# Early values, later weights and filler transposes in the first batch of a pooled-attention and two-MoE kernel

## Chip, cores and metric

The kernel runs on one core of a Trainium2 chip. The metric is the device time of one execution in microseconds; the median of three runs is given. The engines are called as in the profile: PE (TensorE), DVE (VectorE), ACT (ScalarE), POOL (GpSimd) and SP, the queue that issues all transfers here.

## What is computed

Three stages follow each other: attention with pooled queries, a two-matrix MoE, and a second MoE with three input matrices. Batch 4, 8 heads, 1152 keys, head size 64; after pooling 576 queries a head.

```python
q_pool = q.reshape(B, H, S // 2, 2, D).mean(axis=3)
attn = softmax(1 / sqrt(D) * q_pool @ k.T)      # per head
x = (attn @ v)                                  # -> (2304, 512)
h = x @ w_in;  x = max(0.01 * h, h) @ w_out     # 512 -> 2048 -> 512
h = max(max(x @ w1, x @ w2), x @ w3)            # 512 -> 768
out = h @ w2_out                                # 768 -> 512
```

All of it is float32. The weights reach the device as 64-bit floats, viewed as pairs of 32-bit integers, and are decoded there.

## The kernel before

**Batches and pairs.** The heads are taken two at a time: 4 batches of 4 pairs, numbered n = 0 to 15. The attention of a batch runs pair by pair; the two MoE stages of a batch (`experts`) run as filling between the key tiles of the next batch's attention, and those of the last batch run alone at the end. So the attention of the first batch (n = 0 to 3, `n < NP`) has no matmuls of an MoE beside it.

**One pair.** A pair has two phases (320 and 256 query columns a head) of nine key tiles. `prep_q` and `prep_k` transpose queries and keys on PE (tiles `psq`, `psk`), and ACT and DVE split them into a rounded and a rest part. `scores` makes one tile of 128 query rows by 1152 keys with 6 matmuls of 384 columns (tile `s`), DVE takes the row maximum (`mx`, L299 to L309), ACT the exponential (`p`, L302, L305, L310). `probs_t` then handles one key tile: it takes a PSUM bank, transposes four 128x128 blocks of `p` into it (tile `pst`) and lets ACT copy the bank to SBUF (`pt`, L352). `probs_m` does the same for the fifth score tile with three transposes (`psf`, copied by DVE at L361). After three key tiles `values` multiplies by v: 12 matmul records on tile `pv`. `evac` scales and stores the result.

**Slots.** A key tile is a slot. `at(slot, ...)` hangs the next pair's scores, preparations and loads on slots of the current one. `load_v` of the next pair stands on the last slot of the first phase; two `v` buffers take turns. Before the change, eight weight chunks (`PRE = 8`) are hung on slots of the first batch with `predecode`.

**Weights.** There are 56 chunks of 512 KB. `decoded` (L546) loads the raw integers (`wraw`, L551) and turns them into floats with four DVE operations (L561, L564, L567, L571), one on ACT (L570) and one on POOL (L574); `split_chunk` splits the result on ACT (L587) and POOL (L588) into tile `wsplit`, of which a copy is stored to DRAM (L596). Later batches, and chunks that were predecoded, load the split copy back (`w`, L610). There are two raw buffers, two buffers for the decoded floats and five for split chunks (`w_p`). The first two raw loads wait for the first `values` (`GATE`).

**Who sets the order.** The code is recorded in program order, and the tile framework's scheduler then orders each engine's instructions; every engine and the SP queue works its list strictly in that order. `on_pe` (L106 to L120, the line of all matmuls and transposes is L109) only keeps the matmuls of one `values` group together.

Of the kernel before, what the change touches and what calls it, by code (L numbers as in the profile page):

```python
# [7 lines left out]
F32 = mybir.dt.float32  # L8
F32R = mybir.dt.float32r
# [13 lines left out]
def kernel(  # L23
# [22 lines left out]
    B, H, S, D = q.shape  # L46
    T = S // 2
    NP = H // 2
    KT = S // 128
    QP = 72  # L50
    QC = T // QP
    KDM = moe_w_in.shape[0] // 128
# [6 lines left out]
    TM = 512  # L59
# [1 line left out]
    TR_ = B * REST  # L61
    PG = 3
    FREE = 2 * NP
    PRE = 8
    scale = 0.5 / float(D) ** 0.5
    NOSYNC = mybir.DependencyInfo(mybir.DependencyClass.NoSync, mybir.DependencyReason.DATA)

# [3 lines left out]
    vs_p = ctx.enter_context(tc.tile_pool(name="vs", bufs=2))  # L71
# [6 lines left out]
    x_p = ctx.enter_context(tc.tile_pool(name="x", bufs=X_BUFS))  # L78
    g_p = ctx.enter_context(tc.tile_pool(name="g", bufs=6))
    acc_p = ctx.enter_context(tc.tile_pool(name="acc", bufs=1))  # L80
# [13 lines left out]
    ident = const.tile([128, 128], F32, name="ident")  # L94
# [11 lines left out]
    def on_pe(f, *args, **kwargs):  # L106


        mm = f(*args, **kwargs)  # L109
        if grouped[0]:  # L110
            for other in between:
                tc.add_manual_dep(mm.ins, other.name, NOSYNC, reason="values of a group stay together")
            between.clear()
        if behind[0] is not None:
            tc.add_manual_dep(mm.ins, behind[0].name, NOSYNC, reason="values of a group stay together")
        if grouped[0]:
            behind[0] = mm.ins
        else:
            between.append(mm.ins)
        return mm  # L120

    def transpose(out, in_, eye):
        return on_pe(nc.tensor.transpose, out, in_, eye)
# [7 lines left out]
    def bank(name):  # L131
        turn[0] += 1
        pool = ps_w["m"] if ps_w and turn[0] % 2 == 0 else ps_m
        return pool.tile([128, 512], F32, tag="m", name=name)
# [13 lines left out]
    def gap(j):  # L148
        return X0 - 64 * j

    def spare_tiles():
        for j in range(2):
            for part in range(2):
                t = g_p.tile([128, 2, TM], F32R, tag="g", name="qspare")
                t = t.rearrange("p a t -> p (a t)")
                nc.gpsimd.memset(t[:, gap(j):gap(j) + 64].bitcast(F32), 0.0)
                spare[j, part] = t
        for j in range(2):
            t = x_p.tile([128, 2, T], F32R, tag="x", name="kspare")
            spare[j] = t.rearrange("p a t -> p (a t)")  # L160
# [4 lines left out]
    def load_pair(n):  # L165
        b, hp = divmod(n, NP)
        h0 = 2 * hp
        qr = raw_p.tile([QP, 2, QC, 2, D], F32, tag="q", name="qraw")
        kr = raw_p.tile([128, 2, KT, D], F32, tag="k", name="kraw")

        def load_q(j0, j1):
            nc.sync.dma_start(
                out=qr[:, j0:j1].rearrange("p h c r d -> p h (c r) d"),
                in_=q[b, h0 + j0:h0 + j1].rearrange("h (p c) d -> p h c d", p=QP),
            )

        def load_k(j0, j1):
            nc.sync.dma_start(out=kr[:, j0:j1], in_=k[b, h0 + j0:h0 + j1].rearrange("h (p c) d -> p h c d", p=128))

        for j0, j1 in ((0, 1), (1, 2)) if n == 0 else ((0, 2),):  # L180
            load_q(j0, j1)
            load_k(j0, j1)
        raws[n] = [qr, kr]

    kts = {}
    vss = {}

    def load_v(n):
        b, hp = divmod(n, NP)
        h0 = 2 * hp  # L190
        vss[n] = vs_p.tile([128, 2, KT, D], F32, tag="v", name="v")
        nc.sync.dma_start(out=vss[n], in_=v[b, h0:h0 + 2].rearrange("h (p c) d -> p h c d", p=128))

    def pool_q(n, j0=0, j1=2):
        qr = raws[n][0][:, j0:j1]
        for e in range(2):
            engine = nc.vector if n == 0 and j0 == 0 else nc.gpsimd
            a = [qr[:, :, e::2, r] for r in range(2)]
            engine.tensor_tensor(out=a[1 - e], in0=a[0], in1=a[1], op=ALU.add)
# [142 lines left out]
    def probs_t(n, ph, kt):  # L342
        g = kt % PG
        if g == 0:
            pts[kt // PG] = pt_p.tile([128, PG, 2 * X0], F32, tag="pt", name="pt")
        w = (X0, T - X0)[ph]
        ps = bank("pst")
        for i in range(4):
            p = ptl[n, ph, i].rearrange("p a b -> p (a b)")
            transpose(ps[:, i * 128:(i + 1) * 128], p[:, kt * 128:(kt + 1) * 128], ident)  # L350
        dst = pts[kt // PG][:, g, 0:2 * w].rearrange("p (j c) -> p j c", j=2)[:, :, 0:256]
        nc.scalar.copy(out=dst, in_=ps.rearrange("p (j c) -> p j c", j=2))  # L352
# [67 lines left out]
    def attention():  # L420
        npair = B * NP
        load_pair(0)
        for j in range(2):
            pool_q(0, j, j + 1)
            prep_q(0, j)
            prep_k(0, j)
            if j == 0:
                for i in range(2):
                    scores(0, 0, i)
                    normalise(0, 0, i)  # L430
        load_v(0)
        load_pair(1)
        spare_tiles()
        for i in range(2, 5):
            scores(0, 0, i)
            normalise(0, 0, i)
        phases = [(n, ph) for n in range(npair) for ph in range(2)]
        todo = {}

        def at(slot, cost, f, *args):  # L440
            todo.setdefault(slot, []).append((f, args, cost))

        def now(slot):
            spent = 0
            for f, args, cost in todo.pop(slot, []):
                f(*args)
                spent += cost
            return spent

        for u, (n, ph) in enumerate(phases):  # L450
            s0 = u * KT
            if u + 1 < len(phases):
                nxt = phases[u + 1]
                for i, s in enumerate((FIRST_AT if n < NP else S_AT)[nxt[1]]):
                    at(s0 + s, QK * 6 * (1 + (i == 4)), scores, *nxt, i)
                    at(s0 + s + 1, 0, normalise, *nxt, i)
            if ph == 0 and n + 2 <= NP:
                at(s0 + 6, 0, load_pair, n + 2)
            if ph == 0 and n + 1 < npair:
                at(s0 + 1, 0, pool_q, n + 1)  # L460
                when = PREP_AT[n + 1 > NP]
                for j in range(2):
                    at(s0 + when[2 * j], TR * 3, prep_q, n + 1, j)
                    at(s0 + when[2 * j + 1], TR * 4, prep_k, n + 1, j)
                at(s0 + 8, 0, load_v, n + 1)
            if ph == 1 and n + 1 < npair:
                if n + 2 < npair and n + 2 > NP:
                    at(s0 + 6, 0, load_pair, n + 2)
            if n < FREE:
                at(s0 + 4, TR * 2, spread, n, ph)  # L470
        if wide:
            for c in range(PRE):
                at(6 + c * (2 * NP * KT - 8) // PRE, 0, predecode, c)

        late = []

        def follow():
            pn, pph, pgr = late.pop()
            values(pn, pph, pgr)
            if pgr == KT // PG - 1:  # L480
                last = pn % NP == NP - 1
                if pph == 0 and last:
                    yield "room"
                evac(pn, pph)
                if pph == 1 and last:
                    yield "batch"
            return PG * 4 * (X0, T - X0)[pph] / 2400 + 0.565

        for s in range(len(phases) * KT):
            n, ph = phases[s // KT]  # L490
            gr, g = divmod(s % KT, PG)
            done = 0
            want = CHAIN
            if s == 2 * NP * KT:
                done += yield from follow()
            probs_t(n, ph, gr * PG + g)
            done += TR * 4
            if g == PG - 1 and ph == 0:
                probs_m(n, gr)
                done += TR * PG  # L500
                want -= TR * PG
            c = now(s)
            if g == 0 and late:
                c += yield from follow()
            done += c
            yield done, max(0, want - c)
            yield 0, None
            if g == PG - 1:
                late.append((n, ph, gr))
        yield from follow()  # L510
        assert not todo
# [137 lines left out]
    class Main:  # L649
        n = TM  # L650
# [11 lines left out]
    class Rest:  # L662
        n = TR_
# [179 lines left out]
```

## Time and profile before

| | |
|---|---|
| median of 3 runs | 1404.29 us (1402.0 to 1404.84) |
| the profiled execution, its own time | 1402.59 us |
| its span, first to last instruction | 1400.8 us |
| PE busy | 1282.2 us (92%) |
| PE weight loads busy | 1025.2 us (73%) |
| DVE busy | 711.9 us (51%) |
| ACT busy | 637.1 us (45%) |
| POOL busy | 362.2 us (26%) |
| mean granted PE clock | 0.959 |

Busy times are means over very different stretches: the first batch's attention (to about 238 us), three batches of attention with an MoE beside them, and the last MoE alone (from about 1156 us). PE's matmuls are pipelined and their ends modelled, so PE being busy is not the same as PE being at its best. The granted clock is 1.0 at 2.4 GHz and 0.5 at 1.2 GHz. The "chain" of a window is followed back from its last instruction, at each step to what released it or to the instruction ahead of it on its engine.

### The profile page before, as it was taken

How to read it: one execution, taken by the hardware profiler on the slowest of the kernel's cores; microseconds unless marked ns; L12 is line 12 of the kernel's file. 1: busy time of each engine (PE TensorE's matmuls, PEld its weight loads, DVE VectorE, ACT ScalarE, POOL GpSimd, SP SyncE). 2: the span in 40 equal slices, each digit the busy share in tenths (PEclk: the TensorE clock that was granted, in tenths of full speed). 3: DMA queues.
4: the chain of work that ended last, by engine and by line, in shares of the span. 5: the costliest groups of instructions: out<-in, count | busy, mean ns of one | idle time of the engine just before them, and what ended most of it. 6: DMA issues, size and time to landing. Idle time of an engine off the chain costs nothing.

```text
span 1400.8 us, 19351 instructions
## 1 busy us (share of the span) xinstructions
PE 1282.2 (92%) x7376; PEld 1025.2 (73%) x7376; DVE 711.9 (51%) x1214; ACT 637.1 (45%) x1253; POOL 362.2 (26%) x322
## 2 busy tenths in 40 slices
PE   5778879798898988999999998999999999999998
PEld 4445547676676777778787887778777879888888
DVE  5684553587888777354645452445545411222110
ACT  5676664554555665454545353454444432112111
POOL 1251111354566655021212001120220002224110
PEclk8889889998998999999999999999999999999999
DMA  3473221555555656353535343453533244333343
GB/s 110 143 234 123 72 72 39 145 179 194 173 197 189 222 204 193 129 155 121 156 119 150 120 151 100 150 149 129 153 112 128 102 147 156 121 135 122 106 135 106
DMA packets 88056, 197.51 MB, mean 141 GB/s; under 512 B 11420, under 2 KB 41884, under 8 KB 87964
## 3 DMA queue, kind: packets, MB, share of 16 engines
q1 hardware_dynamic: 87964, 196.28, 43.7%
q8 instruction: 58, 0.95, 0.3%
q14 instruction: 34, 0.28, 0.1%
HBM read 150.99 MB, written 35.13 MB: 133 GB/s over the span
## 4 chain that ended last, share of the span: by engine, by line
PE 70%; DVE 11%; DMA 6%; ACT 5%; issue 4%; POOL 4%; SPq 0%; POOLq 0%; DVEq 0%; ACTq 0%
PE m L109 38%; PE pv L109 10%; PE s L109 9%; PE pst L109 6%; PE o L109 5%; DMA wraw<-in_moe_w_out_dram 3%; DVE mx L309 2%; POOL wmant L574 2%; DMA qraw<-in_q_dram 1%; DVE wraw L564 1%; DMA wraw<-in_moe_w_in_dram 1%; POOL wsplit L588 1%; DVE wmant L561 1%; DVE wmant L567 1%; DVE q L253 1%
## 5 line engine op out<-in xcount | busy, mean ns | idle before, releaser
L109 PE MATMUL m<-x,w 128*128 128x512 f32 x1272 | 321.4, 397 | 0.0
L109 PEld LDWEIGHTS m<-x,w 128*128 128x128 f32 x1272 | 231.6, 188 | 56.3 <-issue 13.6
L352 ACT COPY pt<-pst 128x512 f32<-128x512 f32 x288 | 166.7, 586 | 193.5 <-PE pst L109 192.6
L109 PE MATMUL s<-kt,q 128*128 128x384 f32 x840 | 189.9, 360 | 31.3 <-ACT p L310 14.9
L309 DVE TENSOR_REDUCE mx<-s 128x1 f32<-128x1152 f32 x108 | 146.3, 1355 | 126.6 <-PE s L109 124.3
L109 PE MATMUL pv<-pt,v 128*64 128x256 f32 (+1 forms) x1152 | 184.6, 461 | 15.3 <-DVE pt L361 14.7
L109 PE MATMUL pst<-ident,p 128*128 128x128 f32 x1152 | 179.5, 280 | 20.8 <-DVE pt L361 7.7
L109 PEld LDWEIGHTS pst<-ident,p 128*128 128x128 f32 x1152 | 140.9, 143 | 59.7 <-issue 11.1
L109 PEld LDWEIGHTS s<-kt,q 128*128 128x128 f32 x840 | 149.7, 196 | 43.4 <-ACT p L310 17.4
L709 POOL TENSOR_TENSOR g<-t,g 128x512 fp32r<-128x512 f32 x64 | 84.1, 1314 | 348.4 <-DVE g L708 348.4
L310 ACT ACTIVATE p<-s,mx 128x1152 f32<-128x1152 f32 x108 | 132.3, 1225 | 89.1 <-DVE mx L309 88.3
L109 PE MATMUL m<-g,w 128*128 128x512 f32 x624 | 163.2, 400 | 0.0
L109 PEld LDWEIGHTS pv<-pt,v 128*64 128x64 f32 x1152 | 81.5, 150 | 86.6 <-issue 35.3
L109 PEld LDWEIGHTS m<-g,w 128*128 128x128 f32 x624 | 112.3, 189 | 27.4 <-issue 7.7
L707 ACT ACTIVATE t<-m 128x512 f32<-128x512 f32 x80 | 44.3, 555 | 132.9 <-PE m L109 132.9
L109 PE MATMUL m<-x,wsplit 128*128 128x512 f32 x360 | 98.0, 412 | 0.5 <-ACT pt L352 0.4
L708 DVE CAST g<-t 128x512 fp32r<-128x512 f32 x64 | 30.7, 480 | 112.5 <-ACT t L707 112.0
L588 POOL TENSOR_TENSOR wsplit<-wmant,wsplit 128x512 fp32r<-128x512 f32 x56 | 77.3, 1384 | 35.1 <-ACT wsplit L587 35.1
L574 POOL TENSOR_TENSOR wmant<-wraw 128x512 f32<-128x512 f32 x56 | 64.5, 1153 | 80.3 <-DVE wraw L571 67.9
L647 POOL TENSOR_TENSOR y<-t,y 128x512 fp32r<-128x512 f32 x24 | 31.4, 1310 | 202.0 <-ACT y L646 202.0
L109 PEld LDWEIGHTS m<-x,wsplit 128*128 128x128 f32 x360 | 67.1, 195 | 18.9 <-issue 4.9
L737 DVE TENSOR_TENSOR t<-m,t 128x512 f32<-128x512 f32 (+1 forms) x60 | 38.2, 636 | 83.7 <-PE m L109 72.7
(92 smaller groups left out, 1549.2 us busy)
## 6 DMA issues: line engine op xcount, KB each, us to landing
w<-w SPq DMA_DIRECT2D x176, 512.0 KB, 3.4
w<-wsplit SPq DMA_DIRECT2D x56, 512.0 KB, 3.6
wraw<-in_moe_w_out_dram SPq DMA_DIRECT2D x22, 512.0 KB, 6.1
v<-in_v_dram SPq DMA_DIRECT2D x16, 576.0 KB, 3.7
wraw<-in_moe_w_dram SPq DMA_DIRECT2D x18, 512.0 KB, 4.7
qraw<-in_q_dram SPq DMA_DIRECT2D x15, 576.0 KB
kraw<-in_k_dram SPq DMA_DIRECT2D x15, 576.0 KB, 5.4
q<-q SPq DMA_DIRECT2D x52, 160.0 KB, 2.7
```

The lines of the kernel that those rows point to most:

```text
L109: mm = f(*args, **kwargs)
L253: nc.vector.scalar_tensor_tensor(out=lo, in0=src, scalar=scale, in1=hi, op0=ALU.mult, op1=ALU.subtract)
L309: nc.vector.tensor_reduce(out=mx[:, 0:1], in_=ps[:, :, 0:SN], axis=AX.XY, op=ALU.max, negate=True)
L310: nc.scalar.activation(out=p, in_=ps[:, :, 0:SN], func=ACTF.Exp, bias=mx[:, 0:1], accum_out=rs[:, i:i + 1])
L352: nc.scalar.copy(out=dst, in_=ps.rearrange("p (j c) -> p j c", j=2))
L574: nc.gpsimd.tensor_tensor(out=mf, in0=low.bitcast(F32), in1=high.bitcast(F32), op=ALU.mult)
L588: nc.gpsimd.tensor_tensor(out=t[:, 1], in0=r, in1=t[:, 0], op=ALU.subtract)
L647: nc.gpsimd.tensor_tensor(out=t[:, 1], in0=src, in1=t[:, 0], op=ALU.subtract)
L707: nc.scalar.activation(out=t, in_=ps[:, 0:k.n], func=ACTF.Prelu, alpha=0.01)
L708: nc.vector.tensor_copy(out=gt[:, 0], in_=t)
L709: nc.gpsimd.tensor_tensor(out=gt[:, 1], in0=t, in1=gt[:, 0], op=ALU.subtract)
L737: nc.vector.tensor_tensor(out=t, in0=ps[:, 0:k.n], in1=t, op=ALU.max)
```

## The change

Three edits. `PRE` becomes 0, so no `predecode` is recorded. The v of pairs 1 to 3 are loaded right behind that of pair 0 at the start; for pairs 2 and 3 they lie in buffers that are not used yet (the MoE accumulator and one x tile), and the slots of the first batch no longer load v except that of pair 4. And in the first batch `probs_t` writes four transposes of the identity into its PSUM bank ahead of the four real ones, which overwrite them.

```diff
-    PRE = 8
+    PRE = 0
...
-        vss[n] = vs_p.tile([128, 2, KT, D], F32, tag="v", name="v")
+        if n == 2:
+            t = acc_p.tile([128, KDM, TM], F32, tag="acc", name="vacc").rearrange("p m t -> p (m t)")
+            vss[n] = t[:, 0:2 * KT * D].rearrange("p (h c d) -> p h c d", h=2, c=KT)
+        elif n == 3:
+            t = x_p.tile([128, 2, T], F32R, tag="x", name="vx").bitcast(F32).rearrange("p a t -> p (a t)")
+            vss[n] = t.rearrange("p (h c d) -> p h c d", h=2, c=KT)
+        else:
+            vss[n] = vs_p.tile([128, 2, KT, D], F32, tag="v", name="v")
...
         ps = bank("pst")
+        if n < NP:
+            for i in range(4):
+                transpose(ps[:, i * 128:(i + 1) * 128], ident, ident)
         for i in range(4):
             p = ptl[n, ph, i].rearrange("p a b -> p (a b)")
             transpose(ps[:, i * 128:(i + 1) * 128], p[:, kt * 128:(kt + 1) * 128], ident)
...
         load_v(0)
         load_pair(1)
+        for n in range(1, NP):
+            load_v(n)
         spare_tiles()
...
-                at(s0 + 8, 0, load_v, n + 1)
+                if n + 1 >= NP:
+                    at(s0 + 8, 0, load_v, n + 1)
```

The lists that the scheduler makes show what moves. First PE, in one of the first batch's pairs between two `values` groups (`pst<-ident,p` are real transposes, `pst<-ident` fillers, `s<-kspare,qspare` scores of the next pair). Before:

```order
L109 MATMUL pv<-pt,v 64x320 x6
L109 MATMUL pst<-ident,p 128x128 x4
L109 MATMUL s_117<-kspare,qspare 128x384 x4
L109 MATMUL s_119<-kspare,qspare 128x384 x2
L109 MATMUL pst<-ident,p 128x128 x8
L109 MATMUL pv<-pt,v 64x256 x6
```

The same place after the change:

```order
L109 MATMUL pv<-pt,vacc 64x320 x6
L109 MATMUL pst<-ident 128x128 x4
L109 MATMUL pst<-ident,p 128x128 x4
L109 MATMUL s_117<-kspare,qspare 128x384 x4
L109 MATMUL s_119<-kspare,qspare 128x384 x2
L109 MATMUL pst<-ident 128x128 x4
L109 MATMUL pst<-ident,p 128x128 x4
L109 MATMUL pst<-ident 128x128 x4
L109 MATMUL pst<-ident,p 128x128 x4
L109 MATMUL pv<-pt,vacc 64x256 x6
```

Each key tile has its fillers directly ahead of its real transposes; the rest keeps its order.

Second, the SP queue in the first batch, where the first pair gives way to the second (lines L551 and L564 load raw weights, L596 and L609 store split ones, L610 loads them back, L172 and L178 load q and k, L258 and L265 copy query halves). Before:

```order
L551 DMA wraw<-in_moe_w_in_dram 128x4x256
L596 DMA w_138<-wsplit 128x1024
L172 DMA qraw<-in_q_dram 72x2x1024
L610 DMA w<-w_132 128x1024
L610 DMA w<-w_133 128x1024
L610 DMA w<-w_134 128x1024
L258 DMA q_126<-q_126 64x640
L596 DMA w_139<-wsplit 128x1024
L258 DMA q_127<-q_127 64x640
L610 DMA w<-w_135 128x1024
L551 DMA wraw<-in_moe_w_in_dram 128x4x256
L178 DMA kraw<-in_k_dram 128x2x576
```

After:

```order
L609 DMA w_136<-wsplit 128x1024
L564 DMA wraw<-in_moe_w_out_dram 128x4x256
L564 DMA wraw<-in_moe_w_in_dram 128x4x256
L199 DMA v<-in_v_dram 128x2x576
L265 DMA q_124<-q_124 64x640
L416 DMA xr_128<-x 256x1x64
L265 DMA q_125<-q_125 64x640
L172 DMA qraw<-in_q_dram 72x2x1024
L265 DMA q_126<-q_126 64x640
L265 DMA q_127<-q_127 64x640
L178 DMA kraw<-in_k_dram 128x2x576
```

Raw loads still stand in the first batch's list, since the scheduler moves those of the MoE forward into free buffers: 9 in place of 12, 5 stores in place of 8, and no split chunk is loaded back in place of 5.

Third, DVE at the end of the first pair's decoding. Before, the tenth and last decode of the first batch stands in the middle of the second pair:

```order
L325 RECIPROCAL sums<-sums 128x4
L561 TENSOR_SCALAR wmant<-wraw 128x512
L564 SCALAR_TENSOR_TENSOR wraw<-wraw,wmant 128x512
L567 TENSOR_SCALAR wmant<-wraw 128x512
L299 TENSOR_REDUCE mx<-s_117 128x1
L300 TENSOR_REDUCE mx<-s_119 128x1
L571 SCALAR_TENSOR_TENSOR wraw<-wraw,wmant 128x512
L361 COPY pt<-psf 128x6x64
```

After, the seventh and last (L574 to L584 are the four operations) ends in the first pair:

```order
L574 TENSOR_SCALAR wmant<-wraw 128x512
L577 SCALAR_TENSOR_TENSOR wraw<-wraw,wmant 128x512
L306 TENSOR_REDUCE mx<-s_118 128x1
L580 TENSOR_SCALAR wmant<-wraw 128x512
L307 TENSOR_REDUCE mx<-s_119 128x1
L306 TENSOR_REDUCE mx<-s_117 128x1
L308 TENSOR_REDUCE mx<-mx 128x1
L584 SCALAR_TENSOR_TENSOR wraw<-wraw,wmant 128x512
L307 TENSOR_REDUCE mx<-s_119 128x1
L330 TENSOR_TENSOR sums<-sums 128x5
```

So ten decodes in the first batch become seven, and 46 behind it become 49.

## Rows read from the trace of the kernel before

**Rows 1.** The page, part 2: granted TensorE clock in 40 slices of 35 us, in tenths.

```profile
PEclk8889889998998999999999999999999999999999
```

**Rows 2.** Busy time of each engine in four stretches, one per pair (granted clock behind it).

```profile
41.00:97.00 56.00, 41.74 (x236) 28.01 (x234) 41.80 (x85) 38.84 (x88) 24.49 (x21) 0.84 0.60 185
97.00:149.00 52.00, 40.54 (x241) 27.86 (x241) 29.30 (x62) 31.84 (x75) 8.74 (x9) 0.86 0.46 151
149.00:196.00 47.00, 37.74 (x235) 26.73 (x235) 24.22 (x53) 29.93 (x72) 5.43 (x6) 0.90 0.22 54
196.00:243.00 47.00, 41.38 (x234) 29.55 (x234) 18.37 (x30) 22.95 (x47) 5.40 (x6) 0.89 0.18 47
```

**Rows 3.** The chain that ended last, by line, windows 41:97, 97:149, 149:196, 196:243.

```profile
by line: DMA wraw<-in_moe_w_out_dram 14.7%; DMA wraw<-in_moe_w_in_dram 8.6%; PE pv L109 8.4%; DVE wraw L571 5.9%; POOL wmant L574 5.5%; issue 4.2%; DVE mx L300 4.2%; PE pst L109 4.1%; DVE wmant L561 3.8%; DVE mx L299 3.5%; DVE wraw L564 3.2
by line: DMA wraw<-in_moe_w_in_dram 18.3%; PE pv L109 13.5%; DMA qraw<-in_q_dram 12.4%; PE s L109 10.5%; PE pst L109 6.8%; DVE mx L299 5.4%; ACT p L302 5.0%; ACT pt L352 4.1%; ACT p L305 3.2%; DVE qspare L253 2.8%; DVE mx L300 2.7%; PE psq 
by line: PE pv L109 22.1%; PE s L109 18.1%; PE pst L109 15.8%; ACT pt L352 8.3%; ACT p L302 5.6%; DVE mx L299 4.1%; ACT p L305 3.4%; DVE q L253 3.1%; ACT kt L214 3.0%; DVE kspare L217 3.0%; ACT q L249 2.7%; ACT kspare L214 2.5%; issue 2.1%;
by line: PE pv L109 29.0%; PE s L109 20.5%; PE pst L109 17.3%; PE m L109 14.2%; DVE mx L309 5.8%; DVE kt L217 2.9%; ACT p L310 2.8%; ACT pt L352 2.5%; ACT kt L214 2.5%; issue 1.1%; DVE pt L361 1.0%; PE psr L109 0.5%; PE psq L109 0.5%; DVEq 
```

**Rows 4.** Pieces of that chain, 149:196 (start us, us, what).

```profile
159.20 1.12 PE pst L109 x4
...
164.55 0.45 PE pst L109 x4
...
166.32 1.76 PE pv L109 x12
...
169.72 0.87 PE pst L109 x8
...
177.40 1.45 PE pv L109 x12
...
178.85 1.02 PE pst L109 x8
```

**Rows 5.** Longest pieces of values on that chain, 149:196 and 196:243.

```profile
148.99 3.14 PE pv L109 x12
...
160.32 2.60 PE pv L109 x12
...
196.09 3.40 PE pv L109 x12
...
207.71 2.79 PE pv L109 x12
...
226.79 2.70 PE pv L109 x12
```

**Rows 6.** TensorE in three neighbouring stretches (PE busy, granted clock).

```profile
219.90:223.30 3.40, 2.69 (x20) 1.00 0.00 0
223.30:226.70 3.40, 1.24 (x6) 1.00 0.00 0
226.80:230.20 3.40, 3.40 (x16) 0.50 0.03 7
```

**Rows 7.** The same stretches, instructions on score tiles s alone.

```profile
219.90:223.30 3.40, 1.32 (x6) 1.01 (x6) 0.60 (x1) 1.30 (x2) 1.00 0.00 0
223.30:226.70 3.40, 1.24 (x6) 1.01 (x6) 0.76 (x1) 1.31 (x2) 1.00 0.00 0
```

**Rows 8.** Line L561, first operation of each weight decode, 0:235 and 235:600.

```profile
L561 DVE TENSOR_SCALAR wmant<-wraw x10: 417/427/1028, 49.9 to 113.5; 128x512 int32<-128x512 int32 x10
...
L561 DVE TENSOR_SCALAR wmant<-wraw x46: 409/428/1499, 258.7 to 545.8; 128x512 int32<-128x512 int32 x46
```

**Rows 9.** VectorE in order of time, 108:117 (in brackets: idle before, releaser).

```profile
113.46 0.43 DVE L561 TENSOR_SCALAR wmant<-wraw 128x512 int32<-128x512 int32 x1 [3.37 <-DMA wraw<-in_moe_w_in_dram]
```

**Rows 10.** Busy time of each engine in the second batch's stretch and the third's.

```profile
238.00:587.30 349.30, 309.00 (x1687) 240.04 (x1686) 256.05 (x372) 194.15 (x356) 175.75 (x144) 0.94 0.55 182
587.30:883.80 296.50, 285.35 (x1664) 229.41 (x1663) 146.22 (x257) 134.08 (x251) 44.40 (x34) 0.99 0.43 136
```

## The prediction, as put on record

> **What bounds the kernel now.** The change touches the first batch and, through the decodes that it moves on, the second; so I read the page's strip of slices first and then only those stretches. The strip shows where the granted clock is below full: under 0.9 in most slices of the first 210 us, then in two single slices (315 and 420 us), never behind that [rows 1]. The fillers can only win something where the clock is low.
>
> I cut the first batch into its four pairs, each from its first group of values to the next pair's. They are about 56, 51.5, 47 and 47 us long. No engine is full in any of them: PE is busy 41.7 of 56 us in the first, 37.7 of 47 us in the third, and its clock is 0.84 to 0.90 [rows 2]. So busy shares don't decide, and I went to the chain of waits.
>
> The chain says two different things [rows 3]. In the first pair it runs through the raw weight loads (14.7 and 8.6%) and the decodes on DVE and POOL; the key tiles' transposes (pst) hold 4.1% of it. In the second a raw load still holds 18.3%, and pst 6.8%. In the third and fourth, where nothing is decoded, PE's own work holds more than half, and pst alone 15.8 and 17.3%. There PE's order is the bound, and what is put into PE's list ahead of a real transpose lengthens it.
>
> **The fillers.** 72 key tiles get four more transposes each. Counted on the chain, the key tiles whose transposes lie on it are 3, 7, 13 and 14 of the 18 of each pair: 37 in all. Their shares in rows 3 agree: 4.1% of 56, 6.8% of 52, 15.8% and 17.3% of 47 us are 2.3, 3.5, 7.4 and 8.1 us [rows 3]. Four transposes in a stream take 0.45 us on the chain, eight 0.87 us, so four more cost 0.44 us [rows 4]. 37 x 0.44 = **16.3 us**. The fillers write the same bank as the real transposes, so they wait for that bank as these do and don't run while PE waits for it; the order puts them directly ahead of the real ones in nearly every slot. The other 35 I take at nothing: they lie where PE waits anyway for ACT or DVE to free a score bank or a transposed bank, and if that cover is gone they cost 0.44 us each. Bounds: 0, if all of them moved into waits, and 72 x 0.44 = 31.7 us. In a slow stretch four transposes took 1.12 us [rows 4], so a filler there costs more than twice; I keep the price at full clock because the next term takes the slow stretches back.
>
> **The clock.** What low clock costs on the chain is seen by comparing the same piece at both levels. Twelve values records of the first phase take 1.76 us at full clock, those of the second 1.45 us [rows 4]. In slow stretches the first kind took 3.14, 2.60, 3.40 and 2.79 us, the second 2.70 us [rows 5]. That is 1.4, 0.8, 1.6, 1.0 and 1.25 us lost, and for the pieces at 159 and 207 us 0.5 us more each, for the transposes ahead of them: some 7 us in two pairs. The second pair, once it waits for no weights, would have what the third has, 2.7 us. About 10 us could be won. Which of it do four fillers a key tile win? The slow stretches at 159 and 207 us began right after PE had done little but transposes and two scores with short waits between, a key tile's among them; there fillers add work at the right place, and I take these (1.3 + 1.5 us) and the second pair's like them (1.3) in full: 4.1 us. Those that hold the values at 149 and 196 us began in a longer wait for ACT, with one key tile near; I take half of 1.4 + 1.6 + 1.4, so 2.2 us. The one at 226.8 us followed a wait for ACT without any key tile: nothing. Together **-6.3 us**. Bounds 0 and -10.
>
> Whether transposes keep the clock up at all can be read from the trace. From 219.9 to 223.3 us PE was busy 2.69 us, only 1.32 us of it scores and the rest transposes, and the clock stayed at 1.00 behind it; from 223.3 to 226.7 us it was busy 1.24 us, all scores, and the clock then fell to 0.50 [rows 6, 7]. The two had nearly the same score time; the transposes made the difference. The Trainium skill (TensorE: Matmul & The Clock Gate, Part 4: PE-mode transpose) states that transposes do not count as PE-busy in the same way and that the full clock does not engage for them. By that this term would be 0 and the sum 6.3 us higher; these two stretches speak against it, though two are few.
>
> **The decodes that leave the second pair.** The order shows that the edit does only part of what it says: the scheduler pulls seven decodes forward, all into the first pair, as before; only three go. The first pair therefore stays as it is. In the second, DVE stood 3.37 us waiting for a raw load with a row maximum queued right behind it [rows 9]; five loads back of split chunks, which go too, ran beside it. Without them I expect the pair to take what the third took: 51.5 - 47.1 = 4.4, so **-4.4 us**. But then its chain is PE's like the third's, with 13 key tiles instead of 7: 6 x 0.44 = **+2.6 us**. Bounds of the first: 0, and the raw load's whole 18.3% of 52 us, -9.5.
>
> **The three decodes that arrive in the second batch.** Of the 56, 10 began before 235 us and 46 behind it [rows 8]. The second batch took 349.3 us, the third, with the same matmuls and no decodes, 296.5 us [rows 10]: 52.8 us for 46, 1.15 us each. Three more: **+3.4 us**. Bounds: 0, since DVE is busy 256 of 349 us and has room, and 3 x 7.6 = 22.8 us, if decodes set the pace (349.3 / 46). I stay near the low one, because PE is busy 309 of the 349 us.
>
> **The early v.** Nothing: they stand in SP's list behind the first pair's q and k and ahead of copies that wait for DVE anyway, no values waited for a v load on the chain, and the buffers they borrow are first needed by the MoE or by nobody in this batch. If the cover failed, the first queries would come later by a load or two at the start; I keep no range for it.
>
> **Sum.** 16.3 + 2.6 - 6.3 - 4.4 + 3.4 = +11.6 us. On the profiled execution's own 1402.6 us that is **1414 us**. The median shown is 1.7 us above that execution, inside the spread of the runs, and I leave that out.
>
> **The rivals.**
>
> *Faster: PE stays at full clock and the fillers fall into waits.* For it: in the first batch PE idles about a fifth of the time, and a few fillers do move ahead of scores in the order. Against it: the chain has 13 and 14 key tiles of 18 on it. If all 10 us of clock come back, the second pair gains 9.5 and only half of the 43 key tiles pay, the sum is 9.5 - 10 - 9.5 + 3.4 = -6.6 us: **1396 us**. It decides at the number of key tiles that pay: with all of that there is a gain below 37 of them (37 x 0.44 = 16.1), and with the second pair at -4.4 us only below 25.
>
> *No change:* the fillers pay in half the key tiles and the clock comes back in part: 9.5 - 6.3 - 4.4 + 3.4 = +2.2 us, **1404 to 1405 us**.
>
> *The clock is not helped.* Fillers at full price and no clock back: 18.9 - 4.4 + 3.4 = +17.9 us, **1420 us**. The rule of the Trainium skill above (TensorE: Matmul & The Clock Gate, Part 4: PE-mode transpose) would lead here too.
>
> *The weights become the bound.* With 49 decodes behind the first batch the MoE waits for them: 22.8 instead of 3.4 us, **1433 us**. Against it: PE waited nowhere for a split chunk in the trace so far.
>
> **How the numbers follow.** Forecast 0.45, clock not helped 0.15, weights 0.05: slower 0.65. Clock full and fillers hidden: faster 0.20. No change 0.15. About 0.2%, 2.8 us, is what a measurement of this kernel can tell from none. The range reaches from the greater part of the faster case, 1398 us, past the unhelped clock with a little of a weight wait, to 1424 us; what is left out is the rest of either. The slower cases' own range is 1408 to 1424 us.
>
> **What would show it.** Right: pairs three and four some 50 us long instead of 47, with pst about 30% of their chain; the second pair near the third; fewer, not zero, slow stretches before 240 us; seven first operations of a decode ahead of the second batch. Wrong: pairs three and four no longer than before with the clock at 1.0 throughout (faster), or the slow stretches where they were (unhelped), or PE waiting for wsplit in the second batch (weights).

## The result and the profile after

The change took 1415.18 us (median of 3 runs, 1414.17 to 1417.83) against 1404.29 us before; the ratio is 1.0094 with a 95% interval of 1.0064 to 1.0123. The profiled execution took 1414.17 us and spans 1412.4 us, 11.6 us more than before.

Where the time came from is told by the stores that end a pair (tile `xr`, one per pair, in the view of SP's queue in order of time). Before:

```profile
91.39 0.60 SPq L406 DMA_DIRECT2D xr<-x  x1
...
143.26 0.56 SPq L406 DMA_DIRECT2D xr<-x  x1
...
190.36 0.56 SPq L406 DMA_DIRECT2D xr<-x  x1
...
238.06 0.56 SPq L406 DMA_DIRECT2D xr<-x  x1
```

The same view after:

```profile
94.50 0.60 SPq L416 DMA_DIRECT2D xr<-x  x1
...
146.88 0.56 SPq L416 DMA_DIRECT2D xr<-x  x1
...
198.17 0.56 SPq L416 DMA_DIRECT2D xr<-x  x1
...
252.71 0.56 SPq L416 DMA_DIRECT2D xr<-x  x1
```

The first pair ends 3.1 us later, the second takes 52.4 us (51.9 before), the third 51.3 (47.1), the fourth 54.5 (47.7). The first batch ends 14.7 us later. Behind it hardly anything moved: busy time by engine in the second and third batch of the change, cut at the same stores, answers to [rows 10]:

```profile
252.70:601.90 349.20, 307.65 (x1687) 240.01 (x1686) 254.50 (x384) 197.46 (x362) 183.86 (x149) 0.94 0.58 186
601.90:895.30 293.40, 284.33 (x1664) 228.83 (x1663) 146.98 (x257) 134.05 (x251) 44.40 (x34) 0.99 0.45 138
```

349.2 us against 349.3, and 293.4 against 296.5. The second batch now decodes 49 chunks and takes no longer. The 3 us of the third batch are no work of the change: over the profiles of all kernels here, that batch takes 293.3 to 296.6 us. Line L574 of the change, the first operation of a decode, in the first 250 us shows the other seven (ten before, [rows 8]):

```profile
L574 DVE TENSOR_SCALAR wmant<-wraw x7: 418/421/535, 50.1 to 81.8; 128x512 int32<-128x512 int32 x7
```

Busy time by engine in the four pairs of the change, cut at the pairs' first values (the fourth, other than in [rows 2], ends at the store), answers to [rows 2]:

```profile
41.00:100.00 59.00, 45.64 (x306) 35.40 (x305) 40.94 (x81) 37.54 (x84) 19.98 (x18) 0.89 0.57 167
100.00:153.00 53.00, 46.60 (x306) 35.09 (x304) 24.09 (x54) 30.25 (x72) 5.44 (x6) 0.90 0.20 49
153.00:205.00 52.00, 45.48 (x314) 35.23 (x316) 25.06 (x54) 30.27 (x74) 5.46 (x6) 0.93 0.16 37
205.00:253.00 48.00, 42.40 (x266) 32.13 (x266) 16.61 (x28) 22.11 (x44) 5.42 (x6) 0.89 0.14 32
```

And the chain by line in these four windows answers to [rows 3]:

```profile
by line: PE pst L109 20.7%; PE pv L109 13.1%; DMA wraw<-in_moe_w_in_dram 12.2%; PE s L109 8.1%; DVE wraw L577 4.9%; issue 4.9%; DVE mx L306 3.6%; DVE wmant L580 3.4%; ACT pt L362 3.0%; DVE mx L307 2.5%; DVE q L260 2.5%; DVE kspare L224 2.3%
by line: PE pst L109 29.5%; PE pv L109 21.5%; PE s L109 17.4%; ACT pt L362 5.4%; DVE qspare L260 2.8%; DVE kt L224 2.6%; ACT qspare L256 2.4%; issue 2.3%; PE psf L109 2.2%; ACT p L309 2.2%; ACT kt L221 2.2%; DVE pt L371 2.1%; DVE mx L306 1.
by line: PE pst L109 30.3%; PE pv L109 19.3%; PE s L109 17.4%; ACT pt L362 6.6%; DVE q L260 2.8%; DVE kspare L224 2.7%; issue 2.5%; ACT q L256 2.5%; PE psf L109 2.3%; ACT p L309 2.3%; ACT kspare L221 2.2%; PE psq L109 2.2%; DVE pt L371 2.2%
by line: PE pst L109 30.0%; PE pv L109 25.3%; PE s L109 17.8%; PE m L109 7.2%; DVE mx L316 5.7%; DVE kt L224 2.9%; ACT p L317 2.8%; ACT kt L221 2.4%; DVE pt L371 2.2%; PE psf L109 1.4%; ACT pt L362 1.2%; issue 1.0%; PE psr L109 0.5%; DVEq L
```

The transposes' share of the chain went from 4.1, 6.8, 15.8 and 17.3% to 20.7, 29.5, 30.3 and 30.0%. In the third pair that is 30.3% of 52 us, 15.8 us, where it was 7.4. The second pair's chain holds no raw load any more. Pieces of the third pair's chain:

```profile
157.34 0.89 PE pst L109 x8
...
161.60 1.32 PE pst L109 x8
...
164.22 1.97 PE pst L109 x8
...
166.19 3.22 PE pv L109 x12
...
173.94 1.77 PE pv L109 x12
...
175.71 1.02 PE pst L109 x8
```

Eight transposes stand where four stood, at 0.89 us where the clock is full. The slow clock did not go away: around 166 us the values take 3.22 us, where the next group takes 1.77, and the eight transposes ahead of them take 1.97 us.

### The profile page after: what moved, and what is told of

Same layout as the page of the kernel before. It is cut to its first block, busy times and chain, and to the rows that moved or that the text cites. A ratio compares the mean times of both kernels' runs of the same rounds, so it can differ in the third digit from the quotient of the medians.

```text
span 1412.4 us, 19915 instructions
## 1 busy us (share of the span) xinstructions
PE 1303.3 (92%) x7664; PEld 1055.2 (75%) x7664; DVE 707.1 (50%) x1214; ACT 638.6 (45%) x1253; POOL 362.6 (26%) x322
## 4 chain that ended last, share of the span: by engine, by line
PE 72%; DVE 9%; DMA 5%; POOL 4%; issue 4%; ACT 4%; SPq 0%; POOLq 0%; DVEq 0%; ACTq 0%
PE m L109 37%; PE pv L109 10%; PE s L109 9%; PE pst L109 9%; PE o L109 5%; DMA wraw<-in_moe_w_out_dram 2%; DVE mx L316 2%; POOL wsplit L601 2%; POOL wmant L587 2%; DMA qraw<-in_q_dram 1%; DVE wraw L577 1%; DMA wraw<-in_moe_w_dram 1%; DVE wmant L574 1%; DVE pt L371 1%; DVE kt L224 1%
## 5 line engine op out<-in xcount | busy, mean ns | idle before, releaser
L109 PE MATMUL m<-x,w 128*128 128x512 f32 x1224 | 309.2, 397 | 0.0
L109 PEld LDWEIGHTS m<-x,w 128*128 128x128 f32 x1224 | 222.8, 188 | 53.9 <-issue 12.8
L109 PE MATMUL pv<-pt,v 128*64 128x320 f32 (+1 forms) x1008 | 155.3, 447 | 16.0 <-DVE pt L371 16.0
L109 PE MATMUL m<-g,w 128*128 128x512 f32 x576 | 149.9, 399 | 0.0
L109 PEld LDWEIGHTS pv<-pt,v 128*64 128x64 f32 x1008 | 69.8, 147 | 75.0 <-issue 25.3
L109 PEld LDWEIGHTS m<-g,w 128*128 128x128 f32 x576 | 103.6, 188 | 24.5 <-issue 6.2
L109 PE MATMUL m<-x,wsplit 128*128 128x512 f32 x408 | 109.3, 408 | 0.6 <-DVE kt L224 0.5
L109 PEld LDWEIGHTS m<-x,wsplit 128*128 128x128 f32 x408 | 75.3, 192 | 21.3 <-issue 5.7
```

## Experiments

Ratios are to before in the same session, on the same chip, since the median of before moved between sessions (1397.8 to 1404.3 us). All eleven kernels are the change or before with the edits shown or named; one of them was timed twice. The times at which a batch or a pair ends come from one profiled execution of each.

| kernel | ratio to before | 95% interval | first batch ends at, us |
|---|---|---|---|
| before | 1 | | 238.1 |
| the change | 1.0094 | 1.0064 to 1.0123 | 252.7 |
| change without fillers | 0.9981 | 0.9959 to 1.0003 | 235.0 |
| before, fillers alone | 1.0138 | 1.0103 to 1.0173 | 256.4 |
| before, PRE = 0 alone | 0.9981 | 0.9964 to 0.9997 | 234.7 |
| before, early v alone | 0.9994 | 0.9972 to 1.0015 | 236.1 |
| change, eight fillers | 1.0241 | 1.0204 to 1.0278 | 270.2 |
| change, matmuls as fillers | 1.0136 | 1.0110 to 1.0163 | 255.3 |
| change, fillers on the first 4 key tiles of a pair | 0.9985, again 0.9984 | 0.9967 to 1.0003, 0.9966 to 1.0003 | 231.7, 231.8 |
| change, fillers on key tiles 5 to 9 of phase one | 1.0072 | 1.0047 to 1.0097 | 244.5 |
| change, fillers on phase two | 1.0020 | 0.9999 to 1.0042 | 237.6 |
| no fillers, raw loads held to the end of the first batch | 1.0079 | 1.0053 to 1.0105 | 225.3 |
| fillers on the first 4 key tiles, decodes in the second pair | 0.9964 | 0.9946 to 0.9983 | 227.9 |

**Each part alone.** The change without fillers:

```diff
-        if n < NP:
-            for i in range(4):
-                transpose(ps[:, i * 128:(i + 1) * 128], ident, ident)
```

> The change without its fillers: early v and no weights recorded in the first batch stay. Theory (the fillers are the loss): the stores that end the four pairs come within 2 us of where they came before (91, 143, 190, 238 us), the second pair 3 to 5 us shorter, 1400 to 1406 us. Rival (the moved weights or the early v are the loss, and the first pair's 3.4 us more come from v loads in the way of the first raw loads): 1409 us or more, with the first pair still near 60 us.

The pairs ended here (SP's queue again):

```profile
91.70 0.60 SPq L413 DMA_DIRECT2D xr<-x  x1
...
140.59 0.56 SPq L413 DMA_DIRECT2D xr<-x  x1
...
187.83 0.56 SPq L413 DMA_DIRECT2D xr<-x  x1
...
234.99 0.56 SPq L413 DMA_DIRECT2D xr<-x  x1
```

The second pair takes 48.9 us instead of 51.9, the batch ends 3.1 us earlier than before and 17.7 us earlier than with fillers. The later stores come 2.5 to 3.1 us earlier than before, a little more than the theory's 2. So the fillers are the loss. Before with the fillers alone (the three lines above put into it):

> The kernel before with the fillers alone. Theory: 37 key tiles on the chain at 0.44 us, less some 6 us of clock, so 1404 + 10 = 1412 to 1418 us, and pairs three and four 51 to 54 us long as in the change. Rival (the other two edits are the loss): within 3 us of 1404.

The loss is there, and larger than the theory gave: 1.38% or 19.4 us over before, where 8 to 14 us were expected (the median, 1416.33 us, lies in the stated range only because before ran faster that time, at 1399.9 us), with pairs three and four at 54.1 and 54.9 us, a little longer than it said. The two edits that are left, first with `PRE = 0` as the only change to before:

> The kernel before with PRE = 0 alone; v is loaded as before and there are no fillers. Theory (what the run without fillers wins is the second pair freed of three decodes): the second pair 48 to 50 us, the store that ends the batch near 235 us, as without fillers; the second batch unchanged at 349 to 351 us; total 2 to 4 us under before. Rival (the early v wins it): within 1 us of before, second pair at 52 us.

It gives all that the run without fillers gave: second pair 49.3 us, second batch 349.7 us, end of the first batch at 234.7 us, ratio 0.9981. Then the early v alone:

> The kernel before with the early v alone (PRE stays 8, no fillers). Theory (no values wait for v): pair ends within 1.5 us of before, total the same within 0.2%. Rival (v loads collide with the raw loads of the second pair, and early v frees them): second pair at 49 us, total 3 us under before.

No difference that can be measured (0.9994); the second pair took 50.5 us, between the two.

**The amount.** Eight fillers a key tile:

```diff
-            for i in range(4):
+            for i in [0, 1, 2, 3] * 2:
```

> The change with eight fillers a key tile in place of four. Theory (each four fillers on the chain cost 0.44 us, and most key tiles are on it): 43 to 55 key tiles pay 0.44 us once more, 19 to 24 us, less up to 8 us for half of the 48 us of slow clock that are left: 1426 to 1440 us. Rival (the loss comes from the place or from falls of the clock, not from the amount; more fillers keep the clock at full rate): at most 1418 us and no slow stretch in pairs two to four.

1432.79 us, as the theory gave: the second four cost 1.47% or 20.6 us over the change, the first four 1.13% or 15.8 us over none (differences of the ratios, each good to 0.4 or 0.5%). The rival that more fillers save time by a full clock is out. Yet the clock did rise. PE's busy time and granted clock, pair by pair, before, in the change without fillers, in the change and with eight fillers:

```profile
0.00:91.40 91.40, 61.49 (x318) 0.86 0.49 149
91.40:143.30 51.90, 40.68 (x236) 0.85 0.49 160
143.30:190.40 47.10, 38.12 (x236) 0.89 0.22 54
190.40:238.10 47.70, 39.32 (x225) 0.86 0.21 53
```

```profile
0.00:92.00 92.00, 61.30 (x319) 0.87 0.50 155
92.00:141.00 49.00, 40.77 (x238) 0.86 0.25 64
141.00:188.00 47.00, 37.20 (x236) 0.93 0.17 40
188.00:235.00 47.00, 39.02 (x224) 0.85 0.19 41
```

```profile
0.00:95.00 95.00, 65.95 (x404) 0.91 0.53 156
95.00:147.00 52.00, 46.67 (x303) 0.87 0.19 44
147.00:198.00 51.00, 44.54 (x307) 0.93 0.18 44
198.00:253.00 55.00, 46.05 (x294) 0.91 0.16 35
```

```profile
0.00:97.00 97.00, 72.51 (x476) 0.96 0.50 151
97.00:152.00 55.00, 49.83 (x374) 0.97 0.18 40
152.00:211.00 59.00, 53.03 (x386) 0.94 0.17 42
211.00:270.00 59.00, 51.60 (x360) 0.94 0.15 33
```

One less the clock, times two, times the length is the time at 1.2 GHz: 65 us before, 58 without fillers, 48 in the change, 25 with eight fillers. Single profiles scatter (58 us in before with the fillers alone), so the same sum over whole executions, from the recorded clock and span of each, is safer: on average 103 us without fillers (ten executions), 92 in the change (three), 98 in before with fillers (four), 74 with eight (four). Time at the low clock is won back, and the fillers cost more than that gives.

**Transposes or matmuls.** Two plain matmuls in place of the four transposes (the tile still holds the real transposes at the end):

```diff
-            for i in range(4):
-                transpose(ps[:, i * 128:(i + 1) * 128], ident, ident)
+            for i in range(2):
+                matmul(out=ps[:, i * 128:(i + 1) * 128], lhsT=ident, rhs=ident, start=True, stop=True)
```

> The change with two plain matmuls of the identity by itself (128 columns, float32) in place of the four filler transposes. Theory (a transpose keeps the clock up like any other work): two such matmuls take 0.40 to 0.46 us of PE as the four transposes do, the first batch ends within 3 us of the change's 252.7 us, with 12 to 17 slow stretches of 3.4 us before its end (the change has 14). Rival (transposes count for less than matmuls in the clock, as the skill's page has it): at most 9 slow stretches, and the batch ends 4 us or more earlier.

```profile
0.00:92.00 92.00, 64.21 (x402) 0.93 0.54 161
92.00:143.00 51.00, 45.00 (x303) 0.93 0.20 47
143.00:197.00 54.00, 47.61 (x306) 0.87 0.16 40
197.00:255.00 58.00, 49.17 (x293) 0.85 0.15 34
```

The same sum gives 51 us at the low clock against the change's 48, and the batch ends 2.6 us later. In the trace two such matmuls leave four records that take 0.61 us together, as four transposes do (0.60); the timed runs are 0.42% over the change, about as much as two intervals allow for. Over whole executions it is 98 us with matmuls (four executions), the same as in before with filler transposes. Plain matmuls of the same PE time did not hold the clock any better. So the statement of the Trainium skill (TensorE: Matmul & The Clock Gate, Part 4: PE-mode transpose) that transposes do not count in the same way is not borne out by these float32 transposes: eight more a key tile cut the slow time by 33 us against none, and matmuls did no better than four.

**The place.** Three runs split the 72 key tiles: `and ph == 0 and kt < 4` (16 of them), `and ph == 1` (36) and `and ph == 0 and kt >= 4` (20) added to the fillers' condition. The first:

> The change with fillers only ahead of the first four key tiles of each pair's first phase, which lay off the chain before, in the stretch where ACT bounds and the clock falls. Theory (fillers there are covered by the waits for ACT): no cost, the slow stretch at the first values of each pair goes in some pairs at 1.5 us each: 1396 to 1404 us, and no slower than the run without fillers. Rival (fillers cost wherever they stand): 16 x 0.44 = 7 us over the run without fillers.

1395.24 us: no cost, as expected, and the first batch ended 3.3 us earlier than without fillers. These 16 key tiles also win as much of the clock as all 72 do: 94 us at the low clock over a whole execution (ten executions) against 103 without fillers and 92 in the change. Timed again:

> The change with fillers ahead of the first four key tiles of each pair alone, timed again in five rounds against before. Theory: 4 to 7 us under before, of which 3 to 4 us are the second pair without decodes and the rest the clock in the first pair; the interval leaves out 1. Rival: what was seen is the spread of runs, within 0.2% of before.

0.9984, and the interval again just holds 1: the theory's 4 to 7 us were too much. Against no fillers at all (0.9981) there is no difference in the ratios, so what the profile shows as 3.3 us is no measured gain. What is shown is that these 16 cost nothing. The second phase:

> The change with fillers ahead of the nine key tiles of each pair's second phase alone, 36 in all, where PE's order is the chain and the clock is at 1.00. Theory (a filler costs where its key tile is on the chain): 27 to 36 of them pay 0.44 us and no clock comes back, so the first batch ends 12 to 16 us later than without fillers (235.0 us), at 247 to 251 us, and the total is 12 to 16 us over the run without fillers. Rival (fillers cost by their number wherever they stand, 17.7 us for 72): 36 / 72 x 17.7 = 9 us, the end of the batch at 243 to 245 us.

Both failed. The batch ended at 237.6 us, 2.6 us later than without fillers; the timed runs give 0.39%, 5.5 us, for 36 key tiles, 0.15 us each (0.03 to 0.27 by the intervals) and not 0.44. PE's waits for a freed score bank in the third pair show the cover, first without fillers, then with those of the second phase (us in total, times, longest):

```profile
PE s L109 <- ACT p L309: 4.1, 3, 1.4
```

```profile
PE s L109 <- ACT p L309: 1.8, 2, 1.4
```

In this pair 2.3 us of waits for ACT are gone, used up by fillers. The three key tiles between two groups of values where PE had no wait did cost 1.3 us (the groups start 5.6 us apart instead of 4.3), 3 x 0.44, but the whole pair grew only from 47.2 to 47.9 us. Some of the low price may also be the clock's, 93 us at the low level over a whole execution (nine executions) against 103 without fillers; the runs don't part the two. The last five key tiles of the first phase:

> The change with fillers ahead of the last five key tiles of each pair's first phase alone, 20 in all: what the two runs with the first four key tiles and with the second phase leave over. The two ended the batch at 231.7 and 237.6 us against 235.0 us without fillers and 252.7 us with all. Theory (the prices by place add up): 252.7 - 235.0 + 3.3 - 2.6 = 18 us, so the batch ends at 248 to 254 us, more than 20 x 0.44 = 9 us, because a slow stretch of the clock moves into the PE-bound middle of each pair. Rival (each key tile pays at most 0.44 us, and the cost of all of them together is more than the sum, since waits that cover some fillers are used up by others): the end at 236 to 244 us.

The end of the batch, 244.5 us, lies between the two, hardly outside the rival's. That is 9.5 us, 20 x 0.48. The timed runs say 0.91% or 12.7 us, 0.64 each (0.40 to 0.87 by the intervals, so 0.44 is not excluded). By pair the profile tells more: with 14 and 7 us less at the low clock the first two pairs change by +0.8 and -0.3 us, and with 7 and 3 us more of it the last two grow by 4.2 and 4.8 us, where five times 0.44 us would be 2.2. Over whole executions these fillers win nothing of the clock (107 us, five executions). Whether the prices add up depends on what is asked: the timed ratios give 0.4 + 5.5 + 12.7 = 18.6 us for the parts and 15.8 for all, the same within their intervals; the single profiles' batch ends give -3.3 + 2.6 + 9.5 = 8.8 and 17.7 for all. That difference of 9 us stays open. Most of it, 6.7 us, lies in the first pair, and the profiled executions are not the medians of their kernels: without fillers it took 1.7 us more than the median, with the first four key tiles 2.0 less, with the second phase 3.6 more, with the last five 3.4 less.

**The decodes.** No fillers, and the first two raw loads held back to the end of the batch:

```diff
-    GATE = 0
+    GATE = 22
```

> The change without fillers, and with the first two raw loads held until the next to last values of the first batch, so that no weight is decoded in the first three pairs. It tells what the seven decodes left in the first pair cost, and whether decodes moved to the second batch are free. Theory (three moved decodes cost nothing there since DVE has room): the first pair 6 to 10 us shorter, and the second batch longer by 0 to 3 us: total 5 to 9 us under the run without fillers. Rival (the first MoE chunks are then late, and each decode costs 1.15 us or more there): the second batch 8 us or more longer than 350 us, no gain.

The first half of the theory holds, the second falls. The first batch ends at 225.3 us, 9.7 us earlier, nearly all of it in the first pair (82.3 instead of 91.7 us). But the second batch, here and without the gate:

```profile
225.30:592.40 367.10, 312.83 (x1693) 243.65 (x1694) 290.37 (x409) 203.65 (x373) 201.21 (x162) 0.93 0.60 194
```

```profile
235.00:585.10 350.10, 307.82 (x1686) 241.22 (x1685) 259.24 (x384) 197.69 (x362) 182.38 (x149) 0.94 0.58 186
```

takes 367.1 us instead of 350.1. Of the seven decodes two now begin in the last 5 us of the first batch (220.6 and 222.8 us) and five behind it; on average each of the seven costs 2.4 us there and cost 1.4 us in the first pair. The timed runs put the price higher still: 0.98% or 13.7 us over the run without fillers for the whole kernel, where this execution, the fastest of six, took 7.1 us more. MoE matmuls now wait for their chunk (PE's waits, 225 to 300 us):

```profile
PE m L109 <- POOL wsplit L598: 2.7, 1, 2.7
PE m L109 <- ACT wsplit L597: 1.8, 1, 1.8
```

These are 4.5 of the 17 us; what the rest went to was not followed. So three decodes more were free, seven more are not. All the profiles bear out the first: the second batch takes 349.4 us on average with 46 decodes (three profiles, 346.5 to 352.4 us) and as much with 49 (ten, 347.5 to 353.2 us). How many are free was not tried. Last, the fillers on the first four key tiles with `GATE = 5`, so that the seven decodes fall into the second pair:

> Fillers ahead of the first four key tiles of each pair only, and the first raw weight loads held until the first pair's values are done, so that the seven decodes of the first batch fall into the second pair. Theory (the decodes cost 9.7 us wherever DVE has to wait for raw loads): the first pair ends near 80 us, the second takes 55 to 58 us, the batch ends within 2 us of 231.7 us and the total is that of the run with the same fillers. Rival (they cost more in the first pair, because the second pair's first loads and preparation run there): the batch ends 4 us or more earlier, at 1391 us or less.

```profile
80.94 0.60 SPq L416 DMA_DIRECT2D xr<-x  x1
...
135.89 1.55 SPq L416 DMA_DIRECT2D xr<-x  x1
...
182.30 0.57 SPq L416 DMA_DIRECT2D xr<-x  x1
...
227.92 0.56 SPq L416 DMA_DIRECT2D xr<-x  x1
```

The first pair ends at 80.9 us, the second takes 55.0 us, as expected; the third and fourth take 46.4 and 45.6 us instead of 47.4 and 47.5, which nobody expected. The batch ends 3.8 us earlier than with the same fillers alone, between the theory (2 us) and the rival (4 us or more), and the total lies above the rival's 1391 us, so neither is settled. At 1393.53 us, 0.9964 (0.9946 to 0.9983), it has the lowest ratio of all. That is clearly below before and below the change; against the same fillers alone (0.9984) the difference is within the intervals.

## Why the prediction was right, and where it was not

The forecast was 1414 us, the measured median 1415.18, the profiled execution's own time 1414.17. Term by term:

- **The fillers with the clock.** Forecast 16.3 + 2.6 - 6.3 = 12.6 us. Measured: in the ratios 15.8 us taken out of the change and 19.4 us put into before, at the end of the batch 17.7 and 18.4 us. Right in kind and sign, 3 to 7 us low. By pair the forecast is 1.3, 3.7, 3.7 and 3.9 us (3, 13, 13 and 14 key tiles, less the clock won there); the change against itself without fillers shows 2.8, 3.5, 4.1 and 7.4 us, so most of the miss lies in the fourth pair.
- **Which key tiles pay.** Here the step failed that read the chain as a price list ("37 key tiles x 0.44"). The key tiles counted on the chain (13 and 14 in pairs three and four) did not pay alike. Those of the second phase, most of which lay on the chain in these pairs, paid 0.15 us each; in the third pair 2.3 us of their fillers went into waits for ACT that a chain, which follows one path, does not show. The last five of the first phase paid about 0.5 to 0.6. Too much for one and too little for the other partly cancelled. The first four of the first phase, which had lain off the chain, were covered.
- **The clock.** It was right that transposes count and that a part of the slow time goes: 58 us without fillers to 48 us in the first batch, where -6.3 us was the price put on it. That price can't be separated in the runs. What was missed is that slow stretches moved: they now lie in the middle of a pair, where the chain is PE's own work (166 us: 3.22 us of values for 1.77), and the fillers in them pay double (164 us: 1.97 us for eight transposes, 0.89 at full clock), though the prediction kept the price at full clock. That is the likely reason for the last five key tiles' price, and the pairs of that run fit it; it was not tested by itself.
- **The second pair without decodes.** Forecast -4.4 us, measured 3.0 us (51.9 to 48.9, the change without fillers). The mechanism was right, and `PRE = 0` alone gives it.
- **The three decodes that move on.** Forecast +3.4 us, measured nothing (349.3 us before, 349.2 in the change, 350.1 without fillers). The mean price of 52.8 us over 46 decodes was the wrong kind of number: three more are free, and seven more cost 17 us together.
- **The early v.** Forecast nothing, measured nothing.
- **The rivals.** "The clock is not helped" (1420 us) is out by the clock itself, though its price for the fillers, 18.9 us, lies nearer to the measured 15.8 to 19.4 than the forecast's 12.6; "the fillers fall into waits" holds for the first four key tiles and in part for the second phase, not for the rest; of "the weights become the bound" a beginning, matmuls that wait for a chunk, shows only in the gated run, with seven decodes more.

That the sum came within 1.2 us is partly luck. At the end of the first batch it was 6.5 us short (+8.2 forecast, +14.7 measured): the fillers were 5.1 us too cheap and the gain of the second pair 1.4 us too large, both the same way. The +3.4 us for the moved decodes, which did not come, made up half of that, and a third batch that took 3 us less, within its spread from profile to profile, the other half.

## What to carry to other kernels

Work that is put ahead of an engine's useful work in its list was free here only where that engine waited for something else next; try it by place, since the chain of waits names the tiles on one path and not the waits close beside it. Dummy work did hold TensorE's clock, but here 10 us less at the low clock cost 15.8 us of the kernel's time, and 23 us less another 20.6; the 16 places that were free won as much clock as all 72. What moving work to another stage costs need not grow evenly: three decodes were free, seven cost 2.4 us each.

## What was not expected of the hardware

Two float32 matmuls of 128 columns and four float32 transposes of 128 columns took PE alike (0.61 and 0.60 us) and held its clock alike (51 and 48 us at the low level in the first batch, each in one profile; 98 and 92 to 98 us over whole executions). And fillers that raise PE's busy time by 24.9 us (178.3 to 203.2 us) took only 10 us off the 58 us at the low clock that the same kernel has without them; doubling them took 23 us more.
